# A first chunk without doubled products, and loads held until the second solve is done

## The chip, the cores and the metric

The kernel runs on one core of a Trainium2 chip. Its engines are TensorE (PE in the profile, its weight loads PEld), VectorE (DVE), ScalarE (ACT), GpSimd (POOL) and SyncE (SP); each works through its own queue of instructions in order, and they wait for each other by semaphores. SP does nothing here but issue DMAs. The metric is the device time of one execution in microseconds (us).

## The reference

A DeltaNet attention block feeds a feed-forward block. All sums are in float32; the weights arrive as float64.

```python
def _attn_ref(q, k, v, beta):          # 4 batches, 8 heads, 768 tokens, 48 dims
    k_n = k / (np.linalg.norm(k, axis=-1, keepdims=True) + 1e-06)
    state = np.zeros((B, H, D, D), dtype=np.float32)
    for t in range(S):
        kt, vt, bt = (k_n[:, :, t], v[:, :, t], beta[:, :, t, None])
        y[:, :, t] = np.einsum('bhd,bhde->bhe', q[:, :, t], state)
        v_old = np.einsum('bhde,bhd->bhe', state, kt)
        state = state + bt[:, :, :, None] * np.einsum('bhd,bhe->bhde', kt, vt - v_old)

def _moe_ref(x, w_in, w_out, alpha):   # 3072 tokens, 384 -> 2048 -> 384
    h = x @ w_in
    g = np.maximum(h, 0.0) + alpha * np.minimum(h, 0.0)
    return g @ w_out
```

## The kernel before

**Tiling.** The recurrence is cut into 12 chunks of 64 tokens (`C`). A step `n` is one chunk of two of the four batches, so there are 24 steps; steps 0 and 1 are the first chunk. Within a step the tokens of one batch lie on partitions 0 to 63 and of the other on 64 to 127, with 8 heads along the free axis. A chunk's recurrence is a triangular system. Its 64 x 64 triangle is cut into blocks of 32 and these, in the first chunk, into blocks of 16 (`LB`).

**The first chunk.** `eliminate_small(0)` inverts the small blocks on VectorE for four steps at once, for steps 0 to 3, and ends in eight 32-wide transposes: four write `turned`, four write `inverse`. `off_products` multiplies blocks of `turned` (scaled by `which` into a free part of `act`, called `x`) with `mid` and leaves the result in two tiles: `diag`, with all 8 heads, and `away`, which holds heads 4 to 7 with the two batches' halves exchanged. `substitute` then runs three times (k = 0, 1, 2) for each of the two steps: 16 small products each, an addition on VectorE after each (`substituted`). At k = 0 and 2 it reads `away` for heads 4 to 7, at k = 1 it reads `diag`. `solve` multiplies with `inv`, which `place_inverse` fills from `inverse`, and gives `us[n]`. `outputs` gives y, `to_ffn` transposes y into the feed-forward's operand `xt`, and from there `ffn_in(0)` can begin (L1088). Between these stand three transposes of later keys (`flipped`, L430, copied by ScalarE at L439).

**Fill.** From then on the feed-forward matmuls of earlier chunks are dealt out between the steps of the recurrence by hand (`alongside`, `weave`), so that TensorE always has work. Ahead of the first chunk, `busy` fills TensorE with products whose results nobody reads.

**Queues.** All five engines run in the order in which the program is written (`manual_schedule`), DMA issues included, so a line's place in the text is its place in the queue. PSUM has three pairs of banks (`p_pair0` to `2`) that `ps_big` hands out in turn, and two single banks (`p_ffn`) for the feed-forward.

**Weights.** `w_in` comes as 12 pieces of 512 KB, as pairs of 32-bit words. Pieces 0 to 5 are staged in `w_out`, pieces 6 and 7 in `space_out`; pieces 8 to 11 reuse the stages of pieces 0, 2, 1 and 3. `fetch_in(n)` issues the DMAs up to piece n - 1. `begin_in(n)` does ScalarE's part of the conversion up to piece n - 1, two instructions a piece (L262, L263). `conv_in` is a generator that does VectorE's part, two instructions a piece (L272, L277), and, before each piece, ScalarE's part of the next ones if it has not been done; `convert(n)` takes n of its steps. `n_in` is 6.

**Names in the profile.** L687 and L689 are the products in `off_products` (L689 are those that are made a second time for `away`), L690 and L693 the copies after them, L732 `substitute`, L752 and L754 `substituted`, L759 `place_inverse`, L910 and L914 `solve`, L931 the copy of y, L1606 `busy`, L169 the loads of q, k and v in whole halves, L197 `load_late`, L246 the weight loads, L885 the first product of steps 2 and 3 (`through_state`), which reads `beside`, written by ScalarE at L458.

## Time and profile before

| | us |
|---|---|
| median of 3 runs (lowest, highest) | 631.27 (630.54, 631.48) |
| profiled execution | 632.44 |
| its span, first to last instruction | 630.7 |
| last addition before `solve(1)`'s result: `u` L914 starts, takes | 41.24, 0.56 |
| first feed-forward matmul (L1088) starts | 44.33 |
| steps 2 and 3 begin (L885) | 55.04 |

In the windows, each line has a stretch of the span, its length, and for each of PE, PEld, DVE, ACT and POOL the busy microseconds and, in brackets, the number of instructions; then the granted TensorE clock as a share of full speed, the mean busy share of the DMA engines, and GB/s. In the timeline a line has the start, the length, engine, line, operation, tile written and tiles read, shape and count; in square brackets the engine's idle time before it and what ended it. "issue" means that nothing in the profile ended it. A number of the busy table counts an engine's instructions over the whole span.

The DMA queue of SP (q1) moves 192-byte rows for q, k and v and 4096-byte rows for the weights; queues 8 and 14 carry instructions, 71 and 25 packets in the span.

### The profile page before, as it was taken

What the parts mean: (1) busy time and instruction counts of PE and PEld (TensorE: products, weight loads), DVE (VectorE), ACT (ScalarE), POOL (GpSimd) and SP (SyncE); (2) the same over time, 40 slices, a digit from 0 to 9 for tenths busy, and PEclk for the clock granted to TensorE, in tenths of its full rate; (3) what the DMA queues carried; (4) which work ended last, traced back from release to release, by engine and by line L of the source; (5) the groups of instructions that cost most, each with busy time, mean ns of one, the idle gap of its engine ahead of it and who ended that gap; (6) DMA issues with size and microseconds to landing.
All of it is one profiled execution on the core that took longest, in us unless ns stands there. A gap on an engine that the chain in (4) does not pass through costs nothing.

```text
span 630.7 us, 21675 instructions
## 1 busy us (share of the span) xinstructions
PE 617.4 (98%) x9116; PEld 545.5 (86%) x9116; DVE 504.0 (80%) x1223; ACT 312.4 (50%) x836; POOL 99.9 (16%) x218
## 2 busy tenths in 40 slices
PE   6989999999999999999999999999999999999997
PEld 5678788566789989989989989989999999999997
DVE  5978999979989988968978868878979579386383
ACT  6878566255544256446345446335356366352230
POOL 7032221010001000000000000000053062061350
PEclk9989999999999999999999999999999999999999
DMA  7958845212252241241341121211220300100100
GB/s 117 301 120 193 242 87 161 41 38 51 44 85 44 56 73 27 54 74 30 51 76 30 39 40 27 53 26 27 46 51 13 62 15 11 30 3 1 26 1 25
DMA packets 145968, 39.26 MB, mean 62 GB/s; under 512 B 139040, under 2 KB 142256, under 8 KB 145872
## 3 DMA queue, kind: packets, MB, share of 16 engines
q1 hardware_dynamic: 144000, 37.40, 29.0%
q8 instruction: 71, 1.16, 0.7%
q10 hardware_dynamic: 1872, 0.49, 0.4%
q14 instruction: 25, 0.20, 0.1%
HBM read 33.14 MB, written 4.72 MB: 60 GB/s over the span
## 4 chain that ended last, share of the span: by engine, by line
PE 87%; DVE 5%; ACT 3%; DMA 2%; issue 1%; SPq 1%; ACTq 0%; DVEq 0%
PE p_ffn L1088 16%; PE p_ffn L1152 10%; PE p_more L1088 8%; PE p_more L1422 8%; PE p_more L1152 8%; PE p_ffn L1131 5%; PE p_more L1338 5%; PE p_ffn L1328 3%; PE p_ffn L1422 3%; PE p_ffn L1333 3%; PE p_pair L885 2%; PE p_pair L923 2%; PE p_pair L809 2%; PE p_pair L910 2%; PE p_pair L502 2%; PE p_pair L867 2%
## 5 line engine op out<-in xcount | busy, mean ns | idle before, releaser
L1088 PE MATMUL p_ffn<-xt,w_in 128*128 128x256 f32 x528 | 123.2, 384 | 0.1
L1088 PEld LDWEIGHTS p_ffn<-xt,w_in 128*128 128x128 f32 x528 | 97.6, 190 | 14.1 <-issue 0.4
L979 ACT COPY xt<-z 32x96 f32<-32x96 f32 x240 | 64.5, 269 | 49.4 <-DVE z L966 46.3
L1088 PE MATMUL p_more<-xt,w_in 128*128 128x256 f32 x240 | 55.7, 382 | 0.0
L1362 POOL TENSOR_TENSOR k_t<-k_t 128x128 f32<-128x128 f32 (+1 forms) x48 | 28.3, 591 | 166.3 <-ACT k_t L1357 163.8
L600 DVE TENSOR_TENSOR block<-block,prod 128x30 f32<-128x30 f32 (+9 forms) x150 | 50.0, 333 | 5.1
L1088 PEld LDWEIGHTS p_more<-xt,w_in 128*128 128x128 f32 x240 | 44.9, 190 | 6.3
L594 DVE TENSOR_TENSOR prod<-block 128x30 f32<-128x30 f32 (+9 forms) x150 | 48.6, 324 | 1.3
L419 POOL TENSOR_TENSOR beta_t<-beta_t,rec 128x8 f32<-128x8 f32 x24 | 6.9, 288 | 231.8 <-DVE rec L413 228.0
L1100 DVE SCALAR_TENSOR_TENSOR act<-act,al_t,p_ffn 128x256 f32<-128x256 f32 x72 | 31.0, 471 | 14.5 <-ACT act L1098 14.4
L826 ACT COPY inv<-p_pair 32x256 f32<-32x256 f32 x30 | 10.9, 363 | 59.2 <-DVE u L914 35.5
L1098 ACT ACTIVATE act<-p_ffn 128x512 f32<-128x512 f32 x36 | 21.4, 594 | 22.7 <-PE p_ffn L1088 22.4
L1362 POOL TENSOR_TENSOR block<-block 128x128 f32<-128x128 f32 (+1 forms) x48 | 27.7, 577 | 12.6 <-ACT block L1357 10.1
L1328 PE MATMUL p_ffn<-xt,w_in 128*128 128x256 f32 x96 | 29.3, 387 | 0.0
L1152 PE MATMUL p_ffn<-w_out,act 128*128 128x192 f32 x160 | 27.7, 327 | 0.0
L914 DVE TENSOR_TENSOR u<-p_pair,wgt 128x384 f32<-128x384 f32 x24 | 13.2, 554 | 16.8 <-PE p_pair L910 9.9
L1152 PEld LDWEIGHTS p_ffn<-w_out,act 128*128 128x128 f32 x160 | 26.2, 190 | 0.3
L1100 DVE SCALAR_TENSOR_TENSOR act<-act,al_t,p_more 128x256 f32<-128x256 f32 x40 | 17.3, 474 | 10.9 <-ACT act L1098 10.7
L895 DVE TENSOR_TENSOR r<-v_raw,p_pair 64x192 f32<-64x192 f32 (+1 forms) x66 | 23.2, 352 | 2.1 <-PE p_pair L885 1.0
L1152 PE MATMUL p_more<-w_out,act 128*128 128x192 f32 x128 | 22.3, 326 | 0.0
L1357 ACT COPY k_t<-p_more 128x512 f32<-128x512 f32 x16 | 9.4, 587 | 25.5 <-PE p_more L1338 18.9
L1422 PE MATMUL p_more<-w_out,act 128*128 128x192 f32 x128 | 21.6, 327 | 0.0
(285 smaller groups left out, 1486.5 us busy)
## 6 DMA issues: line engine op xcount, KB each, us to landing
w_out<-in_moe_w_in_dram SPq DMA_DIRECT2D x10, 512.0 KB, 5.6
v_raw<-in_v_dram SPq DMA_DIRECT2D x48, 96.0 KB, 2.9
kl<-in_k_dram SPq DMA_DIRECT2D x96, 48.0 KB, 2.4
out_dram<-o_sb SPq DMA_DIRECT2D x90, 48.0 KB, 1.6
space_out<-in_moe_w_out_dram SPq DMA_DIRECT2D x11, 384.0 KB, 4.0
ke_last<-in_k_dram SPq DMA_DIRECT2D x25, 96.0 KB, 3.5
qp<-in_q_dram SPq DMA_DIRECT2D x64, 32.0 KB, 2.2
w_out<-in_moe_w_out_dram SPq DMA_DIRECT2D x5, 384.0 KB, 5.3
```

What stands on the lines that cost most here:

```text
L594: nc.vector.tensor_tensor(out=prod, in0=r[:, 0:j, j : j + 1].to_broadcast([128, j, n]), in1=r[:, j : j + 1, j + 1 : HB].to_broadcast([128, ...
L600: nc.vector.tensor_tensor(out=r[:, 0:j, j + 1 : HB], in0=r[:, 0:j, j + 1 : HB], in1=prod, op=ALU.add)
L895: nc.vector.tensor_tensor(out=r[to, a], in0=v_in[to, a], in1=p[own, a, :, 0:D], op=ALU.subtract)
L979: nc.scalar.copy(to[quad(r), u, bp, t], z[quad(2 * t + u), r])
L1088: nc.tensor.matmul(p_h[:, i], w_in[:, t, (f + i) * 128 : (f + i + 1) * 128], xt[:, t], start=(t == 0), stop=(t == KT - 1),)
L1100: nc.vector.scalar_tensor_tensor(out=g[:, i], in0=g[:, i], scalar=al_t[:, f + i : f + i + 1], in1=p_h[:, i], op0=ALU.mult, op1=ALU.add,)
L1131: nc.tensor.matmul(p_o[u], gs[f // 2][:, f % 2, u * 128 : (u + 1) * 128], w_out[:, f], start=(f == 0), stop=(f == FT - 1),)
L1152: nc.tensor.matmul(p, x(i), w(i), start=(i == 0), stop=(i == FP - 1))
L1328: nc.tensor.matmul(p[:, f * 256 : f * 256 + 256], w(2, f), xt[:, 2], start=True, stop=False)
L1338: nc.tensor.matmul(q[:, j], a, b, start=True, stop=True)
L1362: nc.gpsimd.tensor_tensor(out=dst, in0=a, in1=b, op=ALU.add)
L1422: nc.tensor.matmul(p, x(i), w(i), start=(i == 0), stop=(i == FP - 1))
```

## The change

In `off_products` the products of heads 4 to 7 are made once, straight into the exchanged half; ScalarE copies `diag` for heads 0 to 3 and `away`, and GpSimd copies heads 4 to 7 of `diag` from `away`. VectorE's two copies into `away` are gone. A new `spread` puts 16 products of 32 x 32 into the warm-up, and `busy` loses half a product. ScalarE's part of the fifth piece moves from before the elimination to after the first addition of k = 0, and the last transpose of `inverse` with `place_inverse(0)` to after the second addition of k = 0. Pieces 6 and 7, q and v of step 2, q of step 3 and the key of step 7 move from before the first chunk to after `solve(1)`: GpSimd copies one word of `us[1]` into the first word of piece 6's stage, so that piece 6's DMA waits for it, and the others stand behind it in SP's queue.

```diff
@@ off_products
-        n = C - LB
-        own, other = [ps_big(), None], ps_big()
-        own[1] = ps_big()
         for i in both:
-            p = own[i][:, 0, 0 : H * n].rearrange("p (b i) -> p b i", b=H)
-            q = (other[:, 0] if i == 0 else own[1][:, 1])[:, 0 : G * n]
-            q = q.rearrange("p (b i) -> p b i", b=G)
-            for b in range(H):
-                for t in range(2):
-                    w, y = x[i][half(t), b], mid[i][half(t), b, LB:C]
-                    nc.tensor.matmul(p[half(t), b], w, y)
-                    if b >= G:
-                        nc.tensor.matmul(q[half(1 - t), b - G], w, y)
-            nc.scalar.copy(diag[i][:, :, LB:C], p)
-            other_.append(q)
-        return [
-            lambda i=i: nc.vector.tensor_copy(out=away[i][:, :, LB:C], in_=other_[i])
-            for i in both
-        ]
+            p = region(None, G * (C - LB), g=G)
+            for g, a, t in quarters():
+                b = a * G + g
+                nc.tensor.matmul(
+                    p[half(t ^ a), a, g], x[i][half(t), b], mid[i][half(t), b, LB:C]
+                )
+            nc.scalar.copy(diag[i][:, 0:G, LB:C], p[:, 0])
+            nc.scalar.copy(away[i][:, :, LB:C], p[:, 1])
+            for t in range(2):
+                nc.gpsimd.tensor_copy(
+                    out=diag[i][half(t), G:, LB:C], in_=away[i][half(1 - t), :, LB:C]
+                )
@@ new
+    def spread(n, by, p):
+        for i in range(n):
+            rows = quad(i % 4)
+            nc.tensor.matmul(p[rows, 0:HB], ident[rows, rows], by[rows, 0, 0:HB])
@@ first_chunk
-        aways = off_products(both)
+        off_products(both)
         for _ in range(PIECES - 1):
             next(inverted)
-        aways[0]()
-        next(inverted)
-        assert next(inverted, None) is None
-        aways[1]()
-        place_inverse(0)
...
                 substituted(i, now_at[i], p, k)
+                if (k, i) == (0, 0):
+                    begin_in(5)
                 if i == 0 and k < 2:
                     now(flipped(NJ + k, ps_one()))
+                if (k, i) == (0, 1):
+                    next(inverted)
+                    assert next(inverted, None) is None
+                    place_inverse(0)
...
         now(solve(1))
+        held_back = spare_words[0:1, 0:1].bitcast(FP32)
+        nc.gpsimd.tensor_copy(out=held_back, in_=us[1][0:1, 0, 0, 0:1])
+        fetch_in(n_in + 1)
+        load_q(2)
+        load_early(NJ + NKE)
+        fetch_in(n_in + 2)
+        load_q(3)
+        load_v(2)
         convert(6)
         for i in both:
             now(outputs(i))
-        load_early(NJ + NKE)
         fetch_in(n_in + 4)
@@ before the first chunk
-    fetch_in(n_in + 2)
...
-    load_v(2)
...
-    for i in range(2):
-        load_q(i + 2)
...
     busy(2, k_late[0], p)
-    busy(BUSY - 3.5, mid[1], p)
+    spread(16, mid[1], [x for x in big if x is not turned_beta][0][:, 1])
+    busy(BUSY - 4, mid[1], p)
     for _ in range(6):
         busy(0.25, mid[1], p)
-    begin_in(5)
+    begin_in(4)
```

More of the change, by code (lines that the diff above doesn't have):

```diff
@@ L676, in off_products @@
             nc.vector.tensor_scalar_mul(x[i][:, :, HB:C], own, which[:, 1:2])
-        n = C - LB
-        own, other = [ps_big(), None], ps_big()
-        own[1] = ps_big()
         for i in both:
-            p = own[i][:, 0, 0 : H * n].rearrange("p (b i) -> p b i", b=H)
-            q = (other[:, 0] if i == 0 else own[1][:, 1])[:, 0 : G * n]
-            q = q.rearrange("p (b i) -> p b i", b=G)
-            for b in range(H):
-                for t in range(2):
-                    w, y = x[i][half(t), b], mid[i][half(t), b, LB:C]
-                    nc.tensor.matmul(p[half(t), b], w, y)
-                    if b >= G:
-                        nc.tensor.matmul(q[half(1 - t), b - G], w, y)
-            nc.scalar.copy(diag[i][:, :, LB:C], p)
-            other_.append(q)
-        return [
-            lambda i=i: nc.vector.tensor_copy(out=away[i][:, :, LB:C], in_=other_[i])
-            for i in both
-        ]
-    other_ = []
+            p = region(None, G * (C - LB), g=G)
[10 more added lines that the diff above has]
+                )
     def off_product(n):
```

## The prediction

> **What bounds the kernel now.** I read the busy table and the slices of the span first, then the windows of the first 60 us, then the timeline where the windows show holes, then the DMA view of the same windows.

> ```profile
> PE 617.4 (98%) x9116; PEld 545.5 (86%) x9116; DVE 504.0 (80%) x1223; ACT 312.4 (50%) x836; POOL 99.9 (16%) x218
> ...
> PE   6989999999999999999999999999999999999997
> ...
> PEclk9989999999999999999999999999999999999999
> ```

> TensorE is busy for 98% of the span, and its only thin slices are the first three. So the end is the moment at which TensorE becomes saturated plus a fixed amount of work. Three windows put that moment into numbers:

> ```profile
> 28.00:44.33 16.33, 13.40 (x472) 11.56 (x471) 12.00 (x29) 10.78 (x26) 4.81 (x8) 0.90 0.67 108
> 44.33:55.04 10.71, 10.71 (x207) 8.63 (x203) 9.06 (x19) 8.64 (x20) 2.59 (x6) 1.00 0.72 176
> 55.04:630.70 575.66, 571.62 (x8200) 510.19 (x8199) 463.94 (x1117) 271.45 (x741) 80.14 (x156) 1.00 0.26 51
> ```

> From 44.33 on, the first feed-forward matmul (L1088), TensorE is covered; before it, in the first chunk, 2.93 us are empty and the mean granted clock is 0.90. A microsecond won before 44.33 reaches the end only if nothing else is late behind it. Finer windows and the timeline show where the hole is:

> ```profile
> 34.00:35.00 1.00, 0.65 (x23) 0.43 (x22) 0.60 (x3) 0.77 (x2) 0.90 (x2) 1.00 0.51 98
> 35.00:36.00 1.00, 0.00 (x0) 0.00 (x0) 0.00 (x0) 0.96 (x4) 1.00 (x2) 1.00 0.56 104
> 37.00:38.00 1.00, 1.00 (x39) 1.00 (x35) 0.89 (x3) 1.00 (x3) 0.00 (x0) 0.50 0.80 151
> ...
> 36.41 0.39 PE L732 MATMUL p_pair<-r,diag 64*64 64x48 f32 x12 [1.77 <-issue]
> 36.88 0.35 DVE L752 TENSOR_TENSOR r<-v_raw,p_pair 128x192 f32<-128x192 f32 x1 [2.28 <-PE p_pair L732]
> ...
> q8 instruction: 2, 0.03, 2.3%
> ```

> TensorE stops for 1.77 us in the middle of one substitution (L732) with no semaphore to blame. VectorE waits 2.28 us for it, and then the clock is 0.50 for about three windows. The last line is from the DMA view of 33.7 to 38.9 us: two packets of 16 KB on queue 8, which all through the run moves about one such block for each 256 TensorE instructions. I read the hole as an instruction block that came late behind the small loads that SP issues without a pause from 15.6 to 40 us.

> [...]

> **The change, part by part.**

> *Products without doubles.* 48 L687/L689 products become 32 (16 fewer, with 64 TensorE instructions), and `spread` adds 16 tiny ones to the warm-up, so the block borders stay within 4 instructions. The warm-up loses one 256-column matmul (two records, about 0.43 us at L1088's pace) and gains 32 tiny records (about 0.5 us): nothing, and it lies under VectorE's transposes. The chain from there:
> - `begin_in(4)` takes one conversion (0.68 + 0.68 us on ScalarE) off the queue, so ScalarE's scaling of the first operand can start when `turned` ends (27.78 + 0.62 = 28.40) and not at 28.72: 0.3 us.
> - The first set of products has 32 records in place of 48: about 0.35 us. Then ScalarE makes two copies of 192 columns (no such row; between VectorE's 0.35 for that shape and ScalarE's 0.48 for 384; I take 0.31) for one of 0.48: +0.15. The second set no longer stands in front of the first substitution. It starts at about 30.3 in place of 31.12, and VectorE's first addition, freed of L693 (0.35 + 0.36), at about 31.1 in place of 32.21: 1.1 us.
> - GpSimd's four new copies cost between 0.37 (0.74 for two, at 53.65) and 0.55 each (1.10 for two, at 49.50): 1.5 to 2.2 us, from about 30.3. They are needed only by k = 1, about 32.0, and otherwise delay `off_blocks` (5.1 us from 31.57), of which nobody is short. Nothing.
> - The last transpose of the inverse (0.65) now stands inside VectorE's chain, and the fifth conversion (1.36) in front of ScalarE's copy of a key: the bank of that copy is reused by the next key's transposes, so TensorE reaches the second k = 1 substitution at about 33.4.

> *Loads held.* Six pieces and not eight stand ahead of the key loads. The weight stream runs at about 1.25 us a piece (512 KB at the 400 GB/s of windows 21 to 27), so the keys are through some 2.5 us earlier, and from about 32 until the gate the DMA engines are empty. I take it that the instruction block then arrives in time or at most 0.6 us late, and that the clock stays up. Walking the chain of additions and masks with the rows of before (0.55, 0.35, 0.42, 0.56) from 31.1 gives the end of u[1] at 38.3 (38.9 with a late block), against 41.24 + 0.56 = 41.80: 3.5 us earlier.

> *What is queued behind that.* ScalarE has the sixth conversion, two squares (0.51 each) and a key copy to do before it can copy y; that puts y at 39.6 and the first feed-forward matmul at about 41.75 in place of 44.33: 2.6 us earlier, the most that can be won.

> *The gate's price.* GpSimd's copy of a word (0.2 us by its smallest rows, L419) and a semaphore open SP at about 38.7. In its queue then stand piece 6, two halves each of q and key, piece 7, q, v, and behind them pieces 8 and 9. SP needs about 0.4 us for a piece and 0.64 for a half (rows from 31 to 40), so piece 7 is issued at 38.7 + 3.1 = 41.8. Three nearest rows for landing: 3.8, 4.6 and 5.4 us (pieces 8, 10 and 9 of before); I take 4.2, between the first two, as it follows short loads like piece 10 into a queue as empty as piece 8's. So it lands at 46.0. ScalarE converts in order and waits for it:

> ```profile
> 46.17 0.69 ACT L263 ACTIVATE space_out<-space_out 128x512 f32<-128x512 f32 x1
> 48.03 0.60 ACT L1098 ACTIVATE act<-p_ffn 128x512 f32<-128x512 f32 x1 [1.17 <-PE p_ffn L1088]
> ...
> 54.46 0.57 ACT L458 COPY beside<-p_pair 112x512 f32<-112x512 f32 x1
> ```

> Before, piece 7 was done at 46.86, ScalarE had 1.17 us to spare, and its next 6.3 us of work (relu to L458, without its waits) end at 55.03, where TensorE's L885 waits for it at 55.04. After, piece 7 is done at 46.0 + 1.36 = 47.4, and L885 can start at 47.4 + 6.3 = 53.6 or so: 1.4 us earlier than before. TensorE itself would be there at 52.4; the difference is what the gate takes back. Piece 8, issued at about 44.7, lands by 50 and is wanted at 50.5. Behind L885 every engine moves with TensorE, whose holes after 55.04 sum to 4.04 us in 575.

> **Sum.** The profiled execution took 632.44 us (span 630.7, 1.74 around it), 1.17 over the median of the runs, 631.27. 632.44 - 1.4 = 631.0 for such an execution; at the median 631.27 - 1.4 = 629.9. Bounds: 628.7 where piece 7 is no limit, and 631.7 with a block 0.6 us late and the 5.4 us landing (-1.4 + 0.6 + 1.2 = +0.4).

> **Rivals.**
> 1. *The gate costs nothing* (piece 7 lands under 3 us after its issue, or ScalarE has more slack): the 2.6 us all count, 628.7. For it: 1.25 us a piece in the long stream. Against: no piece of before landed under 3.8 us.
> 2. *The held pieces arrive so late that the kernel is slower.* Packets of piece 9 of before took 46 to 48.9 us, about 2.5 us a piece and not 1.25. With 2.5 for pieces 6 and 7, 1.5 for each 192 KB pair and 0.9 behind, piece 7 lands at 38.7 + 1.0 + 8.0 + 0.9 = 48.6 and L885 moves to 56.2; piece 8, behind two more pairs, comes about 1 us late as well: 57.2, which is 2.2 us after 55.04: 633.4. It decides from a landing after 47.4. For it: each isolated piece of before was slow to start. Against: the small loads overlap with it there.
> 3. *The hole is not undone* (not a late block, or late all the same since the chain runs faster towards the border): the 1.77 us stay, and of the halved stretch the 0.3 or so that VectorE's chain does not cover; u[1] ends 2.1 us later, near 40.4, and the gate moves with it: 631.27 - 1.4 + 2.1 = 632.0. For it: keys and k_late still move at 29 to 32 us, when the block is asked for. Against: the queue is shorter by 1 MB.

> A clock drop near 40 us, where TensorE would rest more than before, halves one stretch of 3.4 us at the start of the matmuls, 1.7 us, of which 1.2 is covered by ScalarE's wait; it is in the range. [...]

> **Chances.** Forecast 0.50, rival 1 0.14, rival 2 0.20, rival 3 0.16. A difference under 0.2% (1.26 us) can't be told from none. The forecast (own range 628.7 to 631.7, the bounds above) is mostly past that: faster 0.35, same 0.15. Rival 1 is faster, rival 2 slower, rival 3 half same, half slower. Together: faster 0.49, same 0.23, slower 0.28. The range from 628.3 to 632.7 leaves out most of rival 2.

> **What would show it.** Right: no hole over 0.6 us in the substitutions, granted clock 1.00 from 34 to 40, u[1] ending near 38.3, L1088 starting near 41.8, ScalarE waiting for DMA before the conversions from space_out, L885 near 53.6. Wrong: a hole without a releaser still there, piece 7 done after 48.8, or L885 gaining what L1088 gained.

## The result and the profile after

| | us |
|---|---|
| median after, 9 runs (lowest, highest) | 634.93 (633.48, 637.48) |
| median before, 9 runs beside them | 631.27 (629.99, 633.46) |
| ratio | 1.0065 [1.0047, 1.0083] |
| profiled execution after, its span | 633.48, 631.7 |

The change makes the kernel 3.7 us slower. The profiled execution after is the fastest of its nine; that of before (632.44) lies 1.2 us above the median of its program. So both programs were profiled a second time, among the experiments below: there before took 630.17 (span 628.5) and after 637.52 (span 635.8).

The page of after, busy table and slices: TensorE still works for 98% of the span, and as many instructions as before, less two.

```profile
PE 617.3 (98%) x9114; PEld 544.1 (86%) x9114; DVE 502.7 (80%) x1221; ACT 312.3 (49%) x838; POOL 101.3 (16%) x223
...
PE   6988999999999999999999999999999999999997
...
PEclk9999999999999999999999999999999999999999
```

The third and fourth slices (31.6 to 63.2 us) are now both an 8; before, the third was an 8 and the fourth a 9. The clock is whole in every slice (0.999 over the span). So the loss is to be looked for in the first tenth of the span, behind the first chunk. The timeline of after shows that the early part came as forecast (first addition, the gate's copy, first feed-forward matmul):

```profile
30.95 0.55 DVE L746 TENSOR_TENSOR r<-v_raw,p_pair 128x384 f32<-128x384 f32 x1 [0.48 <-PE p_pair L724]
...
38.45 0.31 POOL L1675 COPY space_out<-u 1x1 f32<-1x1 f32 x1 [1.58 <-DVE u L906]
...
41.66 1.13 PE L1080 MATMUL p_ffn<-xt,w_in 128*128 128x256 f32 x4
```

(L746 is L754 of before, L906 is L914, L1080 is L1088, L877 is L885, L724 is L732; below, L699 is L707, L902 is L910, L1090 is L1098 and L1092 is L1100. L502 has the same number in both: the products of later keys with themselves.) Then the pieces that were held. The timeline of SP's queue in after; a line is one or two issues, with SP's time for them:

```profile
38.79 0.33 SPq L246 DMA_DIRECT2D space_out<-in_moe_w_in_dram  x1
39.22 1.48 SPq L169 DMA_DIRECT2D qp<-in_q_dram  x2
40.80 1.28 SPq L169 DMA_DIRECT2D ke_pair<-in_k_dram  x2
42.13 0.61 SPq L246 DMA_DIRECT2D space_out<-in_moe_w_in_dram  x1
```

and what ScalarE and TensorE wait for after it:

```profile
43.27 0.68 ACT L262 ACTIVATE w_in<-space_out 128x512 uint32<-128x512 uint32 x1 [1.66 <-DMA space_out<-in_moe_w_in_dram]
...
48.07 0.67 ACT L262 ACTIVATE w_in<-space_out 128x512 uint32<-128x512 uint32 x1 [3.41 <-DMA space_out<-in_moe_w_in_dram]
48.77 0.66 ACT L263 ACTIVATE space_out<-space_out 128x512 f32<-128x512 f32 x1
49.34 0.58 ACT L1090 ACTIVATE act<-p_ffn 128x512 f32<-128x512 f32 x1
49.81 0.47 ACT L699 COPY diag<-p_pair 128x384 f32<-128x384 f32 x1
...
50.34 0.65 PE L430 MATMUL p_pair<-ident,qp 128*112 128x128 f32 x4 [1.05 <-ACT diag L699]
...
55.41 1.00 PE L877 MATMUL p_pair<-beside,k_t 48*64 48x112 f32 x32 [0.25 <-ACT beside L458]
```

Piece 6 lands 4.4 us after its issue (43.19), piece 7 5.9 us after (48.05). ScalarE works in order, so while it waits 3.41 us for piece 7 the relu (L1090) and the copy L699 stand behind the conversion, and TensorE waits for L699 at 50.34 and for L458 at 55.41. (The view of the tile `space_out` gives 4.4 and 5.9 us from issue to landing.)

**Where the time goes.** The windows of the second profile of before (`before_again`) and of after, in the same four stretches (columns as explained above; the last two are the DMA share and GB/s). Before:

```profile
32.00:38.50 6.50, 5.49 (x232) 4.69 (x233) 4.70 (x13) 5.54 (x14) 3.79 (x7) 1.00 0.59 96
38.50:48.00 9.50, 9.01 (x238) 7.31 (x231) 8.98 (x18) 6.01 (x12) 0.86 (x2) 1.00 0.68 170
48.00:58.00 10.00, 10.00 (x246) 8.39 (x248) 7.71 (x21) 9.32 (x27) 2.43 (x7) 1.00 0.79 178
58.00:80.00 22.00, 21.77 (x498) 17.98 (x490) 21.29 (x54) 13.09 (x28) 5.02 (x12) 1.00 0.80 223
```

After:

```profile
32.00:38.50 6.50, 5.49 (x236) 4.60 (x227) 5.67 (x15) 5.27 (x14) 4.60 (x9) 1.00 0.03 6
38.50:48.00 9.50, 8.61 (x191) 6.96 (x192) 8.86 (x18) 3.86 (x8) 0.26 (x1) 1.00 0.86 192
48.00:58.00 10.00, 8.56 (x217) 7.13 (x216) 4.63 (x12) 9.72 (x24) 2.22 (x6) 1.00 0.82 219
58.00:80.00 22.00, 21.44 (x498) 17.22 (x496) 20.93 (x55) 14.15 (x33) 4.65 (x12) 1.00 0.93 247
```

From 32 to 38.5 the DMA engines of after move next to nothing (0.03, against 0.59), and then they are busier in every stretch up to 80 us. TensorE pays between 48 and 58: 8.56 us busy of 10.00. With TensorE's instructions of after laid beside the same ones of that profile of before, after is 0.86 us behind at the transposes of q (L430), 1.06 at L877, 2.68 at the first L502 behind it (61.67 against 58.99), 2.86 at L915 (79 us), and 3.2 at the end. In the second profile of after the same places are 2.35, 2.55, 4.17, 6.83 and 7.3 us behind.

So most of the loss of after is there by 61.67, before any load of `w_out` has landed (the first lands at 66.40). What carries it there is the feed-forward's next relu, which stands behind L458 in ScalarE's queue; ScalarE does its first half (L1090), VectorE its second (L1092). The first half and VectorE's wait for it, in after:

```profile
55.26 0.59 ACT L1090 ACTIVATE act<-p_ffn 128x512 f32<-128x512 f32 x1
...
55.89 0.87 DVE L1092 SCALAR_TENSOR_TENSOR act<-act,al_t,p_ffn 128x256 f32<-128x256 f32 x2 [2.49 <-ACT act L1090]
```

and VectorE in before_again:

```profile
53.21 0.87 DVE L1100 SCALAR_TENSOR_TENSOR act<-act,al_t,p_ffn 128x256 f32<-128x256 f32 x2 [2.06 <-ACT act L1098]
```

From there VectorE works without a pause until L502 can start: it is 2.68 us late at this row, and L502 is 2.68 us late. TensorE itself was only 1.06 late at L877.

### The profile page after: what moved, and what is told of

Same layout as the page of the kernel before. It is cut to its first block, busy times and chain, and to the rows that moved or that the text cites. A ratio compares the mean times of both kernels' runs of the same rounds, so it can differ in the third digit from the quotient of the medians.

```text
span 631.7 us, 21677 instructions
## 1 busy us (share of the span) xinstructions
PE 617.3 (98%) x9114; PEld 544.1 (86%) x9114; DVE 502.7 (80%) x1221; ACT 312.3 (49%) x838; POOL 101.3 (16%) x223
## 4 chain that ended last, share of the span: by engine, by line
PE 88%; DVE 7%; ACT 2%; issue 1%; DMA 1%; POOL 0%; ACTq 0%; DVEq 0%; POOLq 0%
PE p_ffn L1080 17%; PE p_ffn L1144 10%; PE p_more L1080 8%; PE p_more L1414 8%; PE p_more L1144 8%; PE p_ffn L1123 5%; PE p_more L1330 5%; PE p_ffn L1320 3%; PE p_ffn L1414 3%; PE p_ffn L1325 3%; PE p_pair L877 2%; PE p_pair L915 2%; PE p_pair L801 2%; PE p_pair L502 2%; PE p_pair L859 2%; PE p_pair L902 1%
## 5 line engine op out<-in xcount | busy, mean ns | idle before, releaser
L1080 PE MATMUL p_ffn<-xt,w_in 128*128 128x256 f32 x528 | 123.1, 384 | 0.1
L1080 PEld LDWEIGHTS p_ffn<-xt,w_in 128*128 128x128 f32 x528 | 97.6, 190 | 14.0 <-ACT inv L771 0.4
L1080 PE MATMUL p_more<-xt,w_in 128*128 128x256 f32 x240 | 55.7, 382 | 0.0
L1080 PEld LDWEIGHTS p_more<-xt,w_in 128*128 128x128 f32 x240 | 44.9, 190 | 6.3
L594 DVE TENSOR_TENSOR prod<-block 128x30 f32<-128x30 f32 (+9 forms) x150 | 48.6, 324 | 1.3
L1092 DVE SCALAR_TENSOR_TENSOR act<-act,al_t,p_ffn 128x256 f32<-128x256 f32 x72 | 31.0, 471 | 17.5 <-ACT act L1090 17.5
L419 POOL TENSOR_TENSOR beta_t<-beta_t,rec 128x8 f32<-128x8 f32 x24 | 7.0, 291 | 231.0 <-DVE rec L413 227.5
L1090 ACT ACTIVATE act<-p_ffn 128x512 f32<-128x512 f32 x36 | 21.4, 595 | 20.3 <-PE p_ffn L1080 20.1
L906 DVE TENSOR_TENSOR u<-p_pair,wgt 128x384 f32<-128x384 f32 x24 | 13.2, 554 | 16.6 <-PE p_pair L902 9.6
L1092 DVE SCALAR_TENSOR_TENSOR act<-act,al_t,p_more 128x256 f32<-128x256 f32 x40 | 17.3, 474 | 10.9 <-ACT act L1090 10.8
L1144 PE MATMUL p_more<-w_out,act 128*128 128x192 f32 x128 | 22.3, 326 | 0.0
L877 PE MATMUL p_pair<-beside,k_t 48*64 48x112 f32 x704 | 21.4, 259 | 0.4 <-ACT beside L458 0.2
```

Of the source, the lines that this page charges most:

```text
L594: nc.vector.tensor_tensor(out=prod, in0=r[:, 0:j, j : j + 1].to_broadcast([128, j, n]), in1=r[:, j : j + 1, j + 1 : HB].to_broadcast([128, ...
L877: nc.tensor.matmul(p[half(t ^ a), a, g], k_t[n][dims(a), g, half(t)], beside[bp][dims(a), t, g])
L1080: nc.tensor.matmul(p_h[:, i], w_in[:, t, (f + i) * 128 : (f + i + 1) * 128], xt[:, t], start=(t == 0), stop=(t == KT - 1),)
L1092: nc.vector.scalar_tensor_tensor(out=g[:, i], in0=g[:, i], scalar=al_t[:, f + i : f + i + 1], in1=p_h[:, i], op0=ALU.mult, op1=ALU.add,)
L1144: nc.tensor.matmul(p, x(i), w(i), start=(i == 0), stop=(i == FP - 1))
```

## The experiments

14 runs in four groups, each beside runs of before on the same chip. Theories: (a) the price is piece 7's place behind q and a key in SP's queue; (b) the price is the holding itself: 1.6 MB (two pieces of 512 KB and six halves of 96 KB) moved from a time in which the DMA engines then stand empty into a queue that has little slack (the key of step 7 already stood behind `solve(1)` in before; with the gate it only waits for it); (c) the change of the products costs or gains something of its own; (d) the hole in before's profile belongs to that execution and not to the kernel.

### The two programs once more, and the two halves of the change

`before_again` and `after_again` are unchanged. `no_gate` is after with every load where before had it; `gate_only` is before with the loads held.

```diff
no_gate (from after)
-        held_back = spare_words[0:1, 0:1].bitcast(FP32)
-        nc.gpsimd.tensor_copy(out=held_back, in_=us[1][0:1, 0, 0, 0:1])
-        fetch_in(n_in + 1)
...
-        load_v(2)
...
+    fetch_in(n_in + 2)
...
+    load_v(2)
...
gate_only (from before): the same lines the other way round
```

> The kernel before, a second execution under the profiler. Its profiled run was 1.2 us over the median of its runs. If the late instruction block is a matter of luck from run to run, the hole of 1.77 us in L732 is smaller or absent here and the time is nearer 630; if it is fixed by the order of instructions and loads, it is there again at 34.6 us with the same length within 0.3 us. Ratio 1.000 +-0.002.

> A second execution of the changed kernel under the profiler, since the first was the fastest of its nine runs (633.48 against a median of 634.93). Theory 1 (the held pieces are late): piece 7 lands still later here than 48.05 us, ScalarE's wait before the second conversion from space_out is over 3.4 us, and its lateness explains the distance between runs; time 634.9 +-0.6. Theory 2 (the loss is elsewhere, in TensorE's instruction blocks or the clock): the wait is the same 3.4 us, and a hole without a releaser or a clock of 0.50 shows up instead.

> The changed kernel with every load back at its old place and no gate; only the products, the warm-up, the fifth conversion and the last transpose stay changed. Theory 1: piece 6 and 7 are there before they are wanted, ScalarE doesn't wait for DMA before 47 us; the late instruction block may come back (1.8 us). Time 629 to 631.5, below the changed kernel by 3 or more. Theory 2 (products, GpSimd copies and the moved conversion cost more than they save): stays at 634 to 636.

> The kernel before with the gate and the held loads alone, products with doubles as before. Theory 1: no hole in the substitutions, u[1] about 1 to 1.5 us later than in the changed kernel, so the gate opens near 40 and everything behind it is later by as much: 635 to 637. Theory 2: no slower than before, 630 to 631.5.

| kernel | median us | ratio to before |
|---|---|---|
| before_again | 631.59 | 1.0000 [0.9978, 1.0021] |
| after_again | 637.51 | 1.0091 [1.0058, 1.0125] |
| no_gate | 631.44 | 0.9996 [0.9980, 1.0012] |
| gate_only | 637.46 | 1.0083 [1.0055, 1.0111] |

By these medians the held loads are the whole loss, and the products give nothing that can be measured. (gate_only's 637.46 lies just above the 635 to 637 expected. In its one profile, 3.0 of the 6.8 us by which it is behind before_again come at a hole without a releaser, 2.18 us at 74.82 with the clock at 0.50 from there for 3.4 us; neither profile of after has a hole over 0.6 us.) (d) stands too. The timeline of before_again at the place of the hole (34.65 to 36.41 in the first profile, with the clock at 0.50 behind it), and then its window:

```profile
34.26 0.39 PE L732 MATMUL p_pair<-r,diag 64*64 64x48 f32 x12 [0.18 <-issue]
```

```profile
35.00:36.00 1.00, 0.93 (x47) 0.83 (x45) 1.00 (x4) 0.94 (x4) 0.88 (x3) 1.00 0.76 141
```

No hole, and clock 1.00: the same program, with the same loads in flight, reaches the end of `u[1]` at 39.41 (41.80 in the first profile) and L1088 at 41.94 (44.33). Of these 2.4 us, 0.5 stand from the start (the first L502 of the span is at 7.28, against 7.80); the rest comes at the hole and behind it. no_gate in its turn has the hole, at the changed line (TensorE's timeline, then its window):

```profile
35.91 0.38 PE L724 MATMUL p_pair<-r,diag 64*64 64x48 f32 x11 [1.61 <-issue]
```

```profile
36.50:39.50 3.00, 3.00 (x87) 2.91 (x80) 2.39 (x7) 2.88 (x7) 0.18 (x1) 0.50 0.76 145
```

after_again shows a second place where the held loads are paid. ScalarE, then TensorE:

```profile
73.97 0.55 ACT L262 ACTIVATE w_out<-space_out 128x384 uint32<-128x384 uint32 x1 [4.08 <-DMA space_out<-in_moe_w_out_dram]
...
76.63 0.67 PE L1080 MATMUL p_ffn<-xt,w_in 128*128 128x256 f32 x2 [1.75 <-DVE act L1092]
```

and the same wait in before_again:

```profile
66.43 0.56 ACT L262 ACTIVATE w_out<-space_out 128x384 uint32<-128x384 uint32 x1 [0.93 <-DMA space_out<-in_moe_w_out_dram]
```

The first load of `w_out` is issued at 63.89 (57.75 in before_again, 61.09 in the first profile of after). The second one, issued at 67.80, lands at 73.94, and the relu that stands behind its conversion (75.00) makes TensorE wait: it is 4.36 us behind before this wait and 6.35 behind it, so 2.0 of the 7.3 us are lost here alone. In the first profile of after ScalarE waits only 1.26 us there, and TensorE's lag hardly grows (2.68 before, 2.85 behind).

### Which loads, and in what order

`swap` puts piece 7 right behind piece 6; `hold_pieces` holds only the two pieces; `hold_small` holds only q, key and v; `early_gate` opens the gate at the second addition of k = 0 (about 32.9 us).

```diff
swap
-        fetch_in(n_in + 1)
+        fetch_in(n_in + 2)
         load_q(2)
         load_early(NJ + NKE)
-        fetch_in(n_in + 2)
hold_pieces: behind the gate only
+        fetch_in(n_in + 2)
hold_small: behind the gate only
+        nc.gpsimd.tensor_copy(out=q_pad[0][0:1, 0, 0:1], in_=us[1][0:1, 0, 0, 0:1])
         load_q(2)
         load_early(NJ + NKE)
         load_q(3)
         load_v(2)
early_gate
                 if (k, i) == (0, 1):
+                    nc.gpsimd.tensor_copy(out=held_back, in_=now_at[1][0:1, 0, 0, 0:1])
+                    fetch_in(n_in + 2)
+                    load_q(2)
...
```

> The changed kernel with piece 7 right behind piece 6 in SP's queue, both still behind the gate; nothing else moves. Theory 1a (piece 7 stands too far back in the queue and ScalarE converts in order): piece 7 lands near 45 in place of 48.05, the second wait of ScalarE falls from 3.4 us to about 1, steps 2 and 3 begin 2 us earlier; but the weights of w_out still come late behind the same amount of loads. Time 632 to 634. Theory 1b (the whole backlog behind the gate decides, whatever its order): no better than the changed kernel, 634.5 to 637, since q and the key of step 7 are now the ones that are late.

> The changed kernel with the gate on the second addition of k = 0 (it ends near 32.7 us) and not on the second solve (38.4), pieces 6 and 7 ahead of the small loads; the key of step 7 stays behind the second solve, as in the kernel before. Theory 1: the loads move in the 6 us in which the DMA engines were empty, piece 7 lands by 39, ScalarE never waits for DMA, and the lead of 2.7 us at the first feed-forward matmul reaches the end: 628.3 to 629.5, faster than both kernels. Theory 2 (the loads themselves slow the instruction blocks): a hole of over 1 us comes back between 34 and 39, and the time is 630.5 to 632.

> The changed kernel with pieces 6 and 7 alone behind the gate; q, v and the key are back at the places they had in the kernel before. Tells which held loads cost. Theory 1a: piece 7 lands near 44.5 and ScalarE waits about 2 us in all, the queue is caught up by 50: 630.5 to 632. Theory 1b: the pieces are what counts, since each stands in front of ScalarE's order: 633 to 635.

> The changed kernel with the small loads alone held (q of steps 2 and 3, the key of step 7, v of step 2, behind GpSimd's copy of the same word into the pad of the first q buffer); pieces 6 and 7 are loaded early, as in the kernel before. Theory 1a: ScalarE doesn't wait for DMA; TensorE's transposes of q wait at most a microsecond: 630 to 632. Theory 1b: SP's queue is as late as in the changed kernel less two pieces (0.8 us of issue and 2.5 us of transfer), 632 to 634.

| kernel | median us | ratio to before |
|---|---|---|
| swap | 638.57 | 1.0106 [1.0074, 1.0138] |
| early_gate | 634.53 | 1.0039 [1.0021, 1.0058] |
| hold_pieces | 632.72 | 1.0021 [1.0002, 1.0040] |
| hold_small | 634.20 | 1.0039 [1.0019, 1.0059] |

(a) falls. In swap piece 7 has landed at 46.15, two microseconds earlier than in after, but the key is late instead, ScalarE then waits 1.97 us for piece 8 (converted from 52.55), and the first load of `w_out` goes out at 63.37:

```profile
47.65 0.62 PE L430 MATMUL p_pair<-ident,ke_pair 128*112 128x128 f32 x4 [1.77 <-DMA ke_pair<-in_k_dram]
```

Whichever load came first behind the gate, one behind it was late: piece 7 in after (landed 48.05), the key and piece 8 in swap. The two part doses bear (b) out: 1.3 us for the pieces alone and 2.8 for the small loads alone, against 3.7 to 5.9 for both (after, after_again, gate_only). The price of hold_small is not ScalarE's wait for pieces 6 and 7, which are on time there; it waits 1.81 us for piece 8, which SP issues behind the small loads (46.63, lands 51.69), and later 3.15 us for the second `w_out` load. In hold_pieces the first `w_out` load goes out at 58.30, close to before.

The relu shows what these have in common. The table has ScalarE's waits for pieces up to that relu, the start of VectorE's half of it, and TensorE's first L502 behind L877:

| kernel | ScalarE waits for pieces | VectorE's half of the relu | L502 | both later than before_again by |
|---|---|---|---|---|
| before_again | none | 53.21 | 58.99 | |
| hold_pieces | 3.10 (6) | 53.92 | 59.70 | 0.71 |
| hold_small | 1.81 (8) | 55.66 | 61.44 | 2.45 |
| after | 1.66 (6), 3.41 (7) | 55.89 | 61.67 | 2.68 |
| swap | 1.58 (6), 1.85 (7), 1.97 (8) | 56.51 | 62.30 | 3.30 |
| gate_only | 2.43 (6), 3.36 (7) | 57.29 | 63.07 | 4.08 |
| after_again | 2.14 (6), 3.82 (7) | 57.38 | 63.16 | 4.17 |

Whichever piece is late, the relu waits behind its conversion, and L502 is late by what the relu is late.

An earlier gate costs less, but its profile (the slowest of its twelve runs, 636.99) shows two long holes that have no releaser, 3.03 us at L902 and 2.19 us at L502 (74.08), each with the clock at 0.50 behind it. The first:

```profile
40.36 0.56 PE L902 MATMUL p_pair<-r,inv 64*64 64x48 f32 x11 [3.03 <-issue]
```

### A gate in between, no gate with another order, and the products alone

`mid_gate` opens at about 34.3 us, between the two `off_blocks`. `pieces_after_q` has no gate; pieces 6 and 7 stand behind q in SP's queue. `products_only` is no_gate without the moved conversion and transpose. `no_spread` is no_gate without the 16 tiny products in the warm-up.

```diff
mid_gate
+                    off_blocks(3, by_pool=True)
+                    nc.gpsimd.tensor_copy(out=held_back, in_=now_at[1][0:1, 0, 0, 0:1])
+                    fetch_in(n_in + 1)
...
+                    off_blocks(2, by_pool=True)
pieces_after_q (from no_gate)
-    fetch_in(n_in + 2)
     cross(0)
...
         load_q(i + 2)
+    fetch_in(n_in + 2)
products_only (from no_gate)
-                if (k, i) == (0, 0):
-                    begin_in(5)
...
-                if (k, i) == (0, 1):
-                    next(inverted)
...
no_spread (from no_gate)
-    spread(16, mid[1], [x for x in big if x is not turned_beta][0][:, 1])
```

> The changed kernel with the gate at about 34.3 us (behind the first half of GpSimd's scaling, on the second addition of k = 0), loads in the changed kernel's order but with the key of step 7 last. Theory 3 (two prices against each other: transfers that pile up later for every us in which the DMA engines stand empty, and instruction blocks that come late while weights move): fewer late loads than with the gate at 38.4, so ScalarE waits under 1 us for piece 7 and the first load of w_out issues near 59; the hole at the solve is there, under 2 us: 631.5 to 634, between the early gate (634.5) and the best of the partial ones (632.7). Rival (the lateness does not depend on the gate's time): 635 to 637.

> The kernel before with the products without doubles, the spread and the half warm-up product alone; the fifth conversion, the last transpose and all loads are at the old places. If the moved conversion and transpose are what eats the gain of the products (the first key copy keeps a bank, 1.07 us of waiting in the run without a gate), this one is 0.5 to 1.5 us below the kernel before: 630 to 631. If the products' gain is lost in VectorE's chain or in late blocks anyway: 631 to 632, no difference.

> The run without a gate, less the 16 tiny products in the warm-up: 64 TensorE instructions fewer ahead of the first chunk, so every block border lies 64 instructions later in the program. Theory 2 (blocks that come late decide the spread from run to run): the hole moves to another instruction, into the second addition round or the first solve, and the time changes by up to 1.8 us either way: 629.5 to 633. If borders don't matter, it equals the run without a gate, 631.4 +-0.5.

> The run without a gate with pieces 6 and 7 moved in SP's queue from ahead of the keys to behind q, with no gate: SP reaches them near 34.5, the DMA engines never stand empty. Theory 3: nothing piles up (the first load of w_out at 58 as in the kernel before), ScalarE waits under 1 us for piece 7, but weights move when the blocks of the solves are asked for: 630.5 to 632.5. If held pieces cost by themselves, 633 to 635.

| kernel | median us | ratio to before |
|---|---|---|
| mid_gate | 632.61 | 1.0026 [1.0009, 1.0042] |
| pieces_after_q | 631.97 | 1.0018 [1.0003, 1.0032] |
| products_only | 631.80 | 1.0008 [0.9995, 1.0021] |
| no_spread | 636.20 | 1.0082 [1.0064, 1.0100] |

None of the four ways of holding the loads for less time or holding fewer of them is better than not holding them. The products alone bring L1088 to 41.65, against 41.94 in before_again: 0.3 us, below what can be told. Its one profile, the slowest of its eleven runs, then loses more than that in a hole of the kind just seen (2.12 us at L502, 70.40). The medians of after_again, swap, early_gate and no_spread miss every range that was expected for them by 1.5 us or more.

no_spread shows that the tiny products are more than filler. Its TensorE is 0.3 us ahead of before_again's at 59 us and 0.2 at 186, and then falls 5.4 us behind it between 242 and 276 us, in small products of later steps (L801), made 200 us behind the edit. TensorE's timeline there:

```profile
243.43 0.22 PE L801 MATMUL p_pair<-inv,mid 32*32 32x32 f32 x2 [1.35 <-issue]
...
270.94 0.25 PE L801 MATMUL p_pair<-diag,right 32*32 32x32 f32 x4 [2.11 <-issue]
```

Behind the second the clock is 0.50 from 272.3 for 3.4 us.

### The tiny products at another place

`late_spread` is no_spread with the 16 tiny products behind `solve(1)`, so that the instructions from there on have the same numbers as in no_gate. `late_after_q` does the same to pieces_after_q.

```diff
         now(solve(1))
+        spread(16, big[0][:, 0])
```

> The change without the gate, as in no_spread, but the 16 tiny products stand behind the second solve of the first chunk and not in the warm-up, so that all borders of TensorE's instruction blocks from 40 us on are where no_gate has them. no_spread was the earliest of all kernels at 95 us (94.59) and lost its 5 us between 242 and 271 us: two stalls without a releaser in the small products of L801, 1.53 and 2.30 us, and a clock of 0.50 after the second. Theory (the place of the borders): both stalls are gone, the end of the first chunk is as in no_spread (L885 near 52.4, the marker near 94.7), the median is 630.6 to 631.6, ratio to before 0.998 to 1.001. Rival (the 64 records in the warm-up do something else, such as holding the clock up or moving a transfer, or the two stalls were a slow execution): 635 to 636.5 again, with the stalls at L801 as before.

> pieces_after_q (the change without the gate, with pieces 6 and 7 behind q in SP's queue) with the 16 tiny products behind the second solve. In pieces_after_q nothing stood in the way early and it gave 631.97 (1.0018). If the weight loads cost nothing as long as SP issues them without a wait, and the borders from 40 us on are unchanged, the median is 630.8 to 632.0, ratio 0.999 to 1.002, and the first load of w_out is issued by 57.5. If holding the pieces back even by a few microseconds of queue costs, ScalarE waits over 2 us for piece 6 or 7 and the ratio is 1.002 or more. If the early part of the first chunk is worth what the profiles show (L885 0.3 us ahead of the second look at before), it is no more than 0.1% faster.

| kernel | median us | ratio to before |
|---|---|---|
| late_spread | 632.19 | 1.0010 [0.9991, 1.0030] |
| late_after_q | 632.76 | 1.0023 [0.9999, 1.0046] |

late_spread lies 0.6 us above the upper end that the theory of the borders gave, and well below the rival's 635. TensorE is whole again where no_spread lost its time. (The tiny products read `ident` here in place of `mid[1]`.) The windows of late_spread:

```profile
235.00:250.00 15.00, 15.00 (x224) 13.44 (x224) 12.76 (x33) 7.24 (x21) 0.74 (x2) 1.00 0.29 46
265.00:276.00 11.00, 11.00 (x205) 9.89 (x204) 5.78 (x16) 3.65 (x9) 0.41 (x2) 1.00 0.49 84
```

But its own profile, the slowest of its twelve runs, has a hole of 1.36 us at the moved products, L1088 comes only at 44.38 and L885 at 56.25, not near 52.4 as in no_spread: the early gain did not repeat. late_after_q issues its first `w_out` load at 55.60, earlier than before_again, ScalarE waits 1.2 us for a piece, and it is no faster; 1.0023 with an interval that just holds 1 leaves open whether the order costs anything. No version, with a gate or without, beats before.

## Why the prediction was wrong

Forecast 629.9, range 628.3 to 632.7; measured 634.93. At L885 the profiled execution is 1.3 us ahead of before's, as forecast (1.4). Of the 5.0 us by which the median was missed, 2.3 are lost behind L885 (from there to the end 577.98 us, against 575.66), and 2.6 lie in the base: before's profile is 1.17 above the median of its program, and after's 1.45 below. By the steps:

- **The base** (under "Sum": "632.44 - 1.4", and at the median "631.27 - 1.4"). This step failed. The sum took the hole and the halved clock out of one execution and then took the same sum off the median. In before_again neither is there, and `u[1]` ends 2.4 us earlier. Of the 3.5 us that the forecast gave the chain up to `u[1]`, 1.0 is left against before_again (38.39 against 39.41), and in after_again nothing (39.51). The reading as a late instruction block is an inference that the place of the hole supports (see the last section), but whether it is late is a matter of the execution: no_gate and products_only have the same products and loads, and only no_gate's profile shows the hole there.
- **Products without doubles** (-1.1). Right in the profile: the first addition at 30.95 (forecast 31.1). Against before_again (31.64) it is 0.7, and 0.3 of it reach L1088 in products_only. ScalarE's copy of 192 columns took 0.32; the 0.31 of the forecast was right, though it lies below both rows that it was put between.
- **The end of u[1], the first feed-forward matmul, the gate's opening** (38.3, 41.75, 38.7): 38.39, 41.66, and piece 6 issued at 38.79. GpSimd's copy took 0.31 and not 0.2.
- **Piece 7's landing** ("I take 4.2, between the first two"). This term failed: it was mis-sized. It took 5.9 us in after and 6.1 in after_again, beyond the 5.4 that was the worst row. It was issued at 42.13 as forecast (41.8), and lands at 48.05 and not at 46.0; it is done at 49.43 and not at 47.4. The forecast took the queue for as empty as piece 8's; here piece 6 and four halves issued from 38.79 on are still moving, the key's second half up to 45.99, which supports this reading; no run isolates it. A row of before nearer to this case was not used: piece 11, issued at 52.61 right behind piece 10, took 6.1 us.
- **L885** (53.6): its first group starts at 53.72, right by two errors. The row of before in which L885 follows the copy L458 at once was read as a wait of this group. But TensorE is busy for 10.71 of the 10.71 us up to it, so it did not wait there, and after shows the group starting before that copy (54.79), which only the second group needs. The 6.3 us of ScalarE's work were sound: behind the measured 49.43 they give 55.7 for the copy's end, which is 55.36, and the second group waits for it until 55.41.
- **"Behind L885 every engine moves with TensorE"**. This step failed. At L877 TensorE is 1.06 us later than in before_again, but ScalarE's relu and with it VectorE are 2.7 later, by the late piece 7, and TensorE has to wait for them: from L877 to the first L502 it needs 7.95 us and not 6.30 (before) or 6.34 (before_again). That is 1.65 of the 2.3 us; the rest comes in small amounts later. SP does not move with TensorE either: before is 2.4 us behind before_again at L502 and only 0.4 at the first `w_out` load (58.11 against 57.75), while after is 3.3 behind at that load and after_again 6.1. In after this cost TensorE 0.2 us at most, in after_again 2.0.
- **Rival 2** (held pieces too late, 633.4, chance 0.20) is what happened, from the landing it named (after 47.4; measured 48.05). Its 633.4 was still 1.5 us short; it put the lateness on L885 and piece 8 (56.2 and 57.2), where the trace has it on the relu. **Rival 1** falls with gate_only. **Rival 3**, the hole, is real in some executions of before and of no_gate; it is not what made the profiled executions of after slow.

What stays open is why the same kernel gives 634.93 in one group of runs and 637.51 in another, while before gives 631.27 and 631.58. In the slower profile TensorE's first L502 of the span is 0.6 us later already (8.14 against 7.53), with the same loads; its clock is 0.50 from 15.7 to 22.5, in the warm-up, as it is in pieces_after_q, which was not slow; and the gate lets piece 6 go 1.1 us later (39.91 against 38.79); at the first `w_out` load it is 2.8. What made the start late is not shown.

## What to carry to other kernels

A gap that nothing in the profile explains may belong to that one execution (here 1.77 us in one profile of before and 0.18 at the same place in the other): look at a second execution of the unchanged kernel before an edit is credited with removing it. The loads that after held back from a time in which the DMA engines then stood empty (0.03 busy from 32 to 38.5 us) made loads late, themselves and those behind them, up to the first load of `w_out` at least (issued 3.3 us later than in before_again, in after_again 6.1); follow the issuing queue that far, and follow the engine that converts in order beyond the first instruction that another engine waits for. And an edit of a few instructions can cost more far behind it than where it stands (no_spread is 0.2 us ahead of before_again at 186 us and falls 5.4 behind it between 242 and 276).
